# Interleaved weight tails, V returned from PSUM by ScalarE, and q spread one unit ahead

## The chip, the cores and the metric

The kernel runs on one core of one Trainium2 chip. The metric is device time in microseconds (us) of one launch. The engines named below are TensorE (PE, its weight loads PEld), VectorE (DVE), ScalarE (ACT), GpSimd (POOL) and SyncE (SP), which issues nearly all loads.

## The reference

One token for each of 8 sequences goes twice through an attention block with a cached K and V and a small MLP block. What matters, shortened:

```python
def _A_ref(x, k_cache, v_cache, wq, wo):        # x: 8 x 1 x 448, caches: 8 x 8 x 4096 x 256, bf16
    q = (x @ wq).reshape(B, 1, 16, 256)         # 2 query heads for each of 8 kv heads
    scores = einsum("bhqd,bhkd->bhqk", q, k) * 256 ** -0.5
    o = einsum("bhqk,bhkd->bhqd", softmax(scores), v)
    return o.reshape(B, 1, 4096) @ wo

def _B_ref(x, w1, w2, w3, w4):
    ...                                         # with one token the shifted part is zero: x1 = x
    return x1 + gelu(layernorm(x1) @ w3) @ w4

for _ in range(2):
    x = x + _A_ref(layernorm(x), k_cache, v_cache, wq, wo)
    x = x + _B_ref(layernorm(x), w1, w2, w3, w4)
```

Both passes use the same caches (268 MB in all) and the same weights. The second pass of a sequence needs its first one complete.

## The kernel before

**Units and chunks.** A unit is a pass (0 or 1), a sequence b (0 to 7) and a pair of kv heads gp (0 to 3). Its K and its V are four chunks each of 1 MB, 128 partitions of 8192 B. `places` holds 17 such chunks (`slots`, NC = 17). A K chunk is transposed in place by DVE in 32x32 blocks (`transpose_k`, L923, three instructions), multiplied with the spread q by PE into the PSUM tile `sc` (`scores`, L938), and goes through the exponential on ScalarE (`exps`, L947) into `p_n`. P is transposed by PE (L990), copied by ScalarE to `psv` (L997), and for each V chunk ScalarE copies the piece it needs to `ptw` (L1129). PE then multiplies it with V and adds up in `o` (`pv`, L1007). Two K chunks that lie in adjacent places are loaded with one 2 MB transfer (L860, rows of 16384 B) and scored by 32 matmuls 256 wide; otherwise there are two transfers of 1 MB (L891) and 64 matmuls 128 wide.

**What stays on the chip between the passes.** Of gp 2 and 3 of one sequence, 14 of 16 chunks stay in their places after pass 0 and are used again in pass 1. The other two are V chunks that go to PSUM: `inner` (unit gp 2, V chunk 1) to the banks `store0` to `store3`, and `part` (gp 3, V chunk 0), of which 6 of 16 rows go to `store4` and the second half of the bank of `sc`, while the rest sits in `rest`. DVE takes them there in pass 0 with block transposes (`away`, L958, and `part_away`, L979), and brings them back in pass 1 (`back`, L965, and `part_back`, L983) at the second K chunk of (1, b, 2). They go back into two K places that were kept free for this: that of K chunk 0 of (1, b, 2) and that of K chunk 2 of (1, b, 3).

**Order.** The list `items` has all chunk uses in order. It is worked through once, in Python, and each engine's instructions come in that order; `manual_schedule` means that nothing reorders them. A period belongs to one sequence b: its pass 1 on gp 3 and gp 2 from the kept chunks, then K and V of other units mixed (`block`), among them the pass 0 of b+1 on gp 2 and 3, and at the end only V chunks (`narrow`, loaded in two halves of 512 KB, L894), for which three places are left. Beside the narrow stretch runs the `chain`: the output projection of the sequence just finished, its MLP, its next q (`project_q`), in small steps given out by `step`. Each period is about 106 us long.

**Loads.** `emit_loads` is called after each item and issues loads on SP's queue in order while there are places. `place_for` looks for adjacent places for two K chunks and holds a load back for a place that is about to be freed (`held`). Eight DMA semaphores are used in turn, so at most eight loads are in flight.

**q.** For each unit pair (pass, b, half of gp), `give_q` calls `spread_q` at the first K chunk: four small matmuls (L370) into `misc`, then four DVE casts (L376) into one of four `qbds`.

**Weights with 448 rows.** 448 is three blocks of 128 rows and 64 more. `load_split` loads the three blocks (L193). The last 64 rows are cut in two halves by columns: the first goes to partitions 0 to 63, the second to 64 to 127, two loads (L913 for the blocks of wq that are loaded anew for `weights("q", rows)`, at three places in mid-run and one at the start; L1048 on SP's and L1049 on ScalarE's queue for the resident `wq_sb` and `w3_sb`). `wblk` and `q_of_block` choose x block 4 or 3, which have the last 64 values of x in the low or the high partitions and zeros in the others. `project_rows` (L350, L358) multiplies.

Of the kernel before, what the change touches and what calls it, by code (L numbers as in the profile page):

```python
# [17 lines left out]
def kernel(  # L18
# [80 lines left out]
    for u in range(2):  # L99
        nc.vector.tensor_reduce(  # L100
            usel[:, 2 * u : 2 * u + 2],
            ident.rearrange("p (k q h) -> p h k q", k=4, h=2)[:, :, :, 2 * u : 2 * u + 2],
            mybir.AxisListType.XY,
            ALU.add,
        )

    fold = consts.tile([128, 8], FP32, name="fold")
# [234 lines left out]

    def project_rows(w_of, half, r0, r1, ps):

        nb = r1 - r0
        for j in range(2):
            for h in range(HH):
                for fc in range(4):
                    w, xi = w_of(2 * h + j, fc)
                    nc.tensor.matmul(  # L350
                        ps[:, (j * HH + h) * nb : (j * HH + h + 1) * nb],
                        w,
                        xb[Bn][:, xi, r0:r1],
                        start=(fc == 0),
                        stop=(fc == 3),
                    )
        for j in range(2):
            nc.vector.tensor_copy(  # L358
                OT2[:, j, HH * half : HH * half + HH, r0:r1],
                ps[:, j * HH * nb : (j + 1) * HH * nb].rearrange("p (h b) -> p h b", b=nb),  # L360
            )

    def spread_q(b, half, qbd):
# [284 lines left out]
    AFTER = 10  # L648

    def block(k, v=None, slow=False):  # L650

        fresh = [(number[v], 1, c) for c in range(4)] if v else []
# [117 lines left out]
    def late(it):  # L770

        n, kv, c = it
        return kv == 0 and paired(n, c) and not (tasks[n][0] == 1 and stays(it))

    used_at = {it: k for k, it in enumerate(items)}
    for it in items:
# [5 lines left out]
    for b in range(Bn):  # L782
        again[(b, keep[0]), 0, 0] = again[(b, inner[0]), *inner[1:]]
        again[(b, keep[1]), 0, 2] = again[(b, part[0]), *part[1:]]
    free_at = [-1] * NC
# [59 lines left out]
    def emit_loads(most=None):  # L845
        n = 0
        while loads and places and n != most:
# [44 lines left out]
            else:  # L892
                for y in range(2):
                    nc.sync.dma_start(  # L894
                        dst[:, 8 * Dh * y : 8 * Dh * (y + 1)], src[:, 8 * Dh * y : 8 * Dh * (y + 1)]
                    )

    def load_weights(dst, kind, c):

        if kind == "o":  # L900
            nc.sync.dma_start(
                dst[:, 0 : WI * D].rearrange("p (h x) -> p h x", x=2 * D),
                A_wo[0 : WI * 128].rearrange("(h p j) d -> p h (j d)", p=128, j=2),
            )
        elif c == 0:
            nc.sync.dma_start(
                dst.rearrange("p (f c) -> p f c", f=2),
                A_wq[0:256, 0:HF].rearrange("(f p) c -> p f c", f=2),
            )
        else:  # L910
            nc.sync.dma_start(dst[:, 0:HF], A_wq[256:384, 0:HF])
            for k in range(2):
                nc.sync.dma_start(  # L913
                    dst[64 * k : 64 * k + 64, HF : HF + HF // 2],
                    A_wq[384:448, HF // 2 * k : HF // 2 * (k + 1)],
                )

# [36 lines left out]

    def away(slot):

        for n in range(4):
            nc.vector.transpose(  # L958
                store[n][:].bitcast(U32), slot[:].bitcast(U32)[:, 512 * n : 512 * n + 512]
            )  # L960

    def back(slot):

        for n in range(4):
            nc.vector.transpose(  # L965
                slot[:].bitcast(U32)[:, 512 * n : 512 * n + 512], store[n][:].bitcast(U32)
            )

    def part_words(slot):

        w = slot[:].bitcast(U32)
        return [
            (sc[:, 256 : 256 + 128 * (PR - 4)], w[:, 512 : 128 * PR]),
            (store[4][:], w[:, 0:512]),
        ]

    def part_away(slot):
        for kept_words, words in part_words(slot):
            nc.vector.transpose(kept_words.bitcast(U32), words)  # L979

    def part_back(slot):
        for kept_words, words in part_words(slot):
            nc.vector.transpose(words, kept_words.bitcast(U32))  # L983

# [56 lines left out]
    x_row = spare[1][:Bn, 256 : 256 + D]  # L1041
    nc.sync.dma_start(x_row, A_x.rearrange("b s d -> (b s) d"))
    emit_loads(2)
    ps0 = rows_to_cols(x_row, Bn)
    nc.vector.tensor_copy(xT[:], ps0)
    emit_loads(5)
    for t, src, cols in ((wq_sb, A_wq[:, HF:], HF), (w3_sb, B_w3, F)):
        nc.sync.dma_start(t[0:64, 3 * cols :], src[384:448, 0 : cols // 2])  # L1048
        nc.scalar.dma_start(t[64:128, 3 * cols :], src[384:448, cols // 2 : cols])  # L1049
    load_split(wq_sb, A_wq[:, HF:], HF)  # L1050
# [40 lines left out]

    def give_q(who):

# [16 lines left out]
        q_of[k] = who  # L1110
        run(spread_q(who[1], who[2], qbds[k]))

# [3 lines left out]
    v_items = [it for it in items if it[1] == 1]  # L1116
    v_next = dict(zip(v_items, v_items[1:]))
    plain = {it for it in v_items if (tasks[it[0]][:2] == (1, Bn - 1)) and tasks[it[0]][2] in free}

# [14 lines left out]
    for idx, it in enumerate(items):  # L1134
# [22 lines left out]
        if kv == 2:  # L1157
# [8 lines left out]
            elif c == 1:  # L1166
# [3 lines left out]
                def q_of_block(c, fc):  # L1170
                    if fc < 3:
                        t, at = (qw[0], fc * HF) if fc < 2 else (qw[1], 0)
                        return t[:, at + 128 * c : at + 128 * c + 128], fc
                    lo = 128 * c < HF // 2
                    at = HF + 128 * c - (0 if lo else HF // 2)
                    return qw[1][:, at : at + 128], 4 if lo else 3

# [4 lines left out]
                )  # L1182
                project_rows(q_of_block, 0, *rows, ps_q)
        elif kv == 0:
# [46 lines left out]
        else:  # L1231
            st = state[ps, b]
            if it in narrow and it[2] == 0 and not alone and any(e["kind"] == "chain" for e in gens):
                alone.append(n)
# [28 lines left out]
            else:  # L1263
                g8 = gp // 2
                if c == 0 and ("o", g8) not in st:
# [4 lines left out]
                if c == 0:  # L1270
                    o_of[n] = st["o", g8]
                o_now = o_of[n]
                if c == 0 and (alone_now or pairs_done.get((ps, b), 0) % 2 == 1):
                    done = pairs_done.get((ps, b), 0) + 1
# [24 lines left out]
                if ps == 0 and inside(it):  # L1299
                    away(slot)  # L1300
                if ps == 0 and halfway(it):
                    part_away(slot)
            if c == 3:
                pairs_done[ps, b] = pairs_done.get((ps, b), 0) + 1
# [15 lines left out]
        emit_loads()  # L1320
        step(idx, it in narrow)
    while gens:
# [159 lines left out]
```

## Time and profile before

| | us |
|---|---|
| median of three runs (lowest, highest) | 1060.6 (1059.31, 1061.72) |
| time of the profiled execution | 1061.44 |
| span of the profiled execution, first to last instruction | 1059.3 |
| PE busy (matmuls) / PEld | 632.2 / 401.6 |
| DVE busy | 617.0 |
| of it K transposes, L923 | 454.2 |
| of it V from PSUM, L965 and L983 | 28.7 |
| of it V to PSUM, L958 and L979 | 28.9 |
| ACT busy | 161.3 |

The span is what the profile covers; the execution's time has 2.1 us around it. Busy shares are means over stretches with different limits: none of the computing engines is above 60%, and the HBM traffic is 422.39 MB in the span. So the page's totals don't tell what sets the time; the slices and single stretches have to be read.

### The profile page before, as it was taken

Reading aid. Unit: us, or ns where it says so; the run is one execution under the profiler, and the core shown is the slowest. Engines: PE = TensorE matmul, PEld = TensorE weight load, DVE = VectorE, ACT = ScalarE, POOL = GpSimd, SP = SyncE. Lnnn points to the kernel's source line nnn. Section 1 sums busy time; section 2 is a strip of 40 time slices with the busy share of each in tenths; the row PEclk is TensorE's granted clock in tenths of the full one; section 3 lists DMA queues with packets and bytes.
Section 4 is the critical chain, followed back from the end, with each engine's and each line's share of the span. In section 5 each row is a group of like instructions: output and inputs, shape, how many; then the busy total and the mean of one; then the engine's idle time right before and its main releaser. Section 6 shows DMA issues by size and latency. Waiting matters only on the chain.

```text
span 1059.3 us, 29997 instructions
## 1 busy us (share of the span) xinstructions
PE 632.2 (60%) x13328; PEld 401.6 (38%) x13328; DVE 617.0 (58%) x1334; ACT 161.3 (15%) x615; POOL 16.3 (2%) x27
## 2 busy tenths in 40 slices
PE   3154454766476657754766576547664865576765
PEld 2032232543244424532434254324332543244544
DVE  5155567259725972597258825872588259724672
ACT  1011011121112121212111112111111121102110
POOL 0000000000000000000000000000000000000000
PEclk9999755775666555665665566757665665576665
DMA  9999999999999999999999999999999999999994
GB/s 303 389 420 424 422 420 420 394 416 423 418 388 416 420 415 332 409 423 419 395 394 420 421 377 410 423 421 404 377 424 422 392 417 422 419 398 392 418 418 187
DMA packets 72768, 424.32 MB, mean 401 GB/s; under 512 B 7608, under 2 KB 13632, under 8 KB 43456
## 3 DMA queue, kind: packets, MB, share of 16 engines
q1 hardware_dynamic: 72448, 422.17, 98.7%
q8 instruction: 104, 1.70, 0.6%
q10 hardware_dynamic: 192, 0.25, 0.1%
q14 instruction: 24, 0.20, 0.0%
HBM read 422.39 MB, written 0.01 MB: 399 GB/s over the span
## 4 chain that ended last, share of the span: by engine, by line
DMA 46%; DVE 26%; PE 21%; ACT 3%; issue 2%; SPq 1%; POOL 1%; DVEq 0%; ACTq 0%
DMA places<-in_A_v_cache_dram 30%; DVE places L923 20%; DMA places<-in_A_k_cache_dram 13%; PE sc L938 7%; PE o L1007 6%; PE misc L174 3%; ACT p_n L947 2%; DMA places<-in_A_wq_dram 2%; DVE store L958 2%; PE misc L529 1%; DVE qbd L376 1%; DMA places<-in_A_wo_dram 1%; DVE places L965 1%; SPq L193 1%; PE misc L350 0%
## 5 line engine op out<-in xcount | busy, mean ns | idle before, releaser
L923 DVE STREAM_TRANSPOSE places<-places 128x512 uint32<-128x512 uint32 (+1 forms) x576 | 454.2, 853 | 75.8 <-DMA places<-in_A_k_cache_dram 74.4
L938 PE MATMUL sc<-places,qbd 128*8 128x256 bf16 (+1 forms) x5344 | 248.4, 333 | 236.3 <-DVE places L923 227.8
L1007 PE MATMUL o<-places,ptw 128*8 128x256 bf16 x3808 | 233.2, 370 | 92.7 <-DMA places<-in_A_v_cache_dram 61.6
L938 PEld LDWEIGHTS <-qbd 128*8 128x8 bf16 x5344 | 134.8, 103 | 319.0 <-DVE places L923 140.8
L1007 PEld LDWEIGHTS <-ptw 128*8 128x8 bf16 x3968 | 103.1, 102 | 162.5 <-issue 83.0
L947 ACT ACTIVATE p_n<-sc 128x256 bf16<-128x256 f32 x128 | 95.2, 744 | 403.8 <-PE sc L938 403.8
L1129 ACT COPY ptw<-psv 128x32 bf16<-128x32 bf16 x248 | 51.9, 226 | 184.9 <-PE o L1007 180.5
L493 DVE RECIPROCAL rz<-misc 128x8 f32<-128x8 f32 (+1 forms) x37 | 6.8, 183 | 89.0 <-PE misc L490 89.0
L529 PE MATMUL misc<-R_t,o_sb 128*128 128x8 f32 (+1 forms) x140 | 29.8, 322 | 40.7 <-DVE R_t L515 35.4
L997 ACT CAST psv<-misc 128x128 bf16<-128x128 f32 x64 | 17.0, 265 | 236.3 <-PE misc L990 236.3
L529 PEld LDWEIGHTS misc<-R_t,o_sb 128*128 128x128 f32 x140 | 26.9, 268 | 51.0 <-issue 40.4
L376 DVE CAST qbd<-misc 32x32 bf16<-32x32 f32 x128 | 23.3, 182 | 37.1 <-PE misc L370 35.6
L947 ACT ACTIVATION_READ_ACCUMULATOR p_n<-sc 128x1 f32 x128 | 33.9, 265 | 0.0
L174 PEld LDWEIGHTS <-w_sb 128*128 128x128 bf16 x896 | 27.1, 100 | 16.5 <-issue 15.8
L525 DVE MEMSET o<- 128x256 f32 x35 | 9.5, 272 | 33.4 <-PE o L1007 30.9
L275 POOL TENSOR_TENSOR t<-t,nhalf 128x2 f32<-128x2 f32 (+2 forms) x18 | 12.0, 669 | 977.9 <-DVE t L296 977.9
L990 PE MATMUL misc<-identb,p_n 128*128 128x32 bf16 x256 | 18.0, 190 | 8.9 <-ACT p_n L947 6.8
L174 PEld LDWEIGHTS <-wo_sb 128*128 128x128 bf16 x704 | 20.9, 100 | 6.4 <-issue 6.4
L990 PEld LDWEIGHTS <-p_n 128*128 128x128 bf16 x256 | 11.8, 104 | 30.2 <-issue 18.7
L958 DVE STREAM_TRANSPOSE store<-places 128x512 uint32<-128x512 uint32 x32 | 19.7, 685 | 0.0
L965 DVE STREAM_TRANSPOSE places<-store 128x512 uint32<-128x512 uint32 x32 | 19.7, 674 | 0.0
L174 PE MATMUL misc<-xb,w_sb 128*128 128x32 bf16 x448 | 16.1, 187 | 4.9 <-DVE xb L304 4.8
(150 smaller groups left out, 348.8 us busy)
## 6 DMA issues: line engine op xcount, KB each, us to landing
places<-in_A_k_cache_dram SPq DMA_DIRECT2D x51, 2048.0 KB, 17.7
places<-in_A_v_cache_dram SPq DMA_DIRECT2D x194, 512.0 KB, 7.2
places<-in_A_k_cache_dram SPq DMA_DIRECT2D x90, 1024.0 KB, 13.4
places<-in_A_v_cache_dram SPq DMA_DIRECT2D x87, 1024.0 KB, 19.9
rest<-in_A_v_cache_dram SPq DMA_DIRECT2D x8, 640.0 KB, 18.4
places<-in_A_wo_dram SPq DMA_DIRECT2D x5, 896.0 KB, 19.7
places<-in_A_wq_dram SPq DMA_DIRECT2D x4, 1024.0 KB, 12.7
places<-in_A_v_cache_dram SPq DMA_DIRECT2D x8, 384.0 KB, 17.5
```

The costliest lines, as they stand in the source:

```text
L174: nc.tensor.matmul(bass.AP(out.tensor, out.offset, [out.ap[0], (1, WIDE)]), w, x.to_broadcast([128, WIDE]), start=start, stop=stop, skip_g ...
L376: nc.vector.tensor_copy(qbd[32 * a : 32 * a + 32, :, :, a, :], qs.rearrange("p e (f g u h) -> p (e f) u g h", f=2, u=2, h=2)[:, :, u],)
L529: nc.tensor.matmul(ot_ps[:, j], o_sb[:].rearrange("p (i j) -> p j i", j=2)[:, j], R, start=True, stop=True)
L923: nc.vector.transpose(w, w)
L938: nc.tensor.matmul(sc[32 * k : 32 * k + 8, 128 * (x % 2) : 128 * (x % 2 + nx)], qbd[:, ep, gp % 2].rearrange("p a h -> p (a h)"), v, start ...
L947: nc.scalar.activation(p_sb[:, :, :, 2 * u : 2 * u + 2].rearrange("p t i x -> p x t i"), sc[:, 0:256].rearrange("p (x t i) -> p x t i", x= ...
L958: nc.vector.transpose(store[n][:].bitcast(U32), slot[:].bitcast(U32)[:, 512 * n : 512 * n + 512])
L965: nc.vector.transpose(slot[:].bitcast(U32)[:, 512 * n : 512 * n + 512], store[n][:].bitcast(U32))
L990: nc.tensor.matmul(pt_ps[:, t], p_sb[:, t].rearrange("p i x -> p (i x)"), cols, start=True, stop=True,)
L997: nc.scalar.copy(p_to, pt_ps.rearrange("p t k (a h) -> p a (t k) h", a=4))
L1007: nc.tensor.matmul(o_ps[32 * q : 32 * q + 8, :], ptz[:, at : at + 8], v[:, y * Dh : (y + 1) * Dh] if v2 is None or y < PR else v2[:, (y - ...
L1129: nc.scalar.copy(ptw[:, ring_of[it], :, 6:8], psv[slot_of[it[0]]][:, it[2]])
```

## The change

Three parts, and what they need.

1. The last 64 rows of a weight are loaded in one transfer to 128 partitions: row r, halved by columns, goes to partitions 2r and 2r+1 (`load_tail`). For wq blocks loaded anew, the 64 values of x are doubled to match: `tail_cols` multiplies with a selector that DVE writes, and DVE masks the two halves by `parity` into `xq`. For the resident `wq_sb` and `w3_sb` the tails are loaded into place 13, and at item 12 PE sorts them into the layout of before, through PSUM, with ScalarE's copies (`sort_tail`). Place 13 joins the others then. x is loaded on ScalarE's queue.
2. `part` and `inner` are kept in PSUM as plain copies (`away`, a DVE bitwise OR with 0 on 32-bit words) and come back by ScalarE copies (`back`), of which one is issued after each item (`move`). They are used as the last V chunk of their units (`v_order`), and return to the places of the first two V chunks of (1, b, 3), no longer to two K places.
3. At the third K chunk of a unit, `q_ahead` issues the matmuls of the next q to be spread, and the casts follow at the fourth.

```diff
+    def tail_cols(r0, r1, ps):
+        nb = r1 - r0
+        two_t = chn.tile([128, Dh], FP32, tag="o_sb")
+        two = two_t[:, 0:64].bitcast(BF16)
+        nc.vector.tensor_copy(
+            two.rearrange("p (r k) -> p r k", k=2),
+            identb[:, 64:128].unsqueeze(2).to_broadcast([128, 64, 2]),
+        )
+        nc.tensor.matmul(ps, two, xb[Bn][:, 3, r0:r1], start=True, stop=True)
+        nc.vector.tensor_tensor(
+            xq[:, :, 0:nb],
+            ps.unsqueeze(1).to_broadcast([128, 2, nb]),
+            parity[:].unsqueeze(2).to_broadcast([128, 2, nb]),
+            ALU.mult,
+        )
+        return lambda xi: xb[Bn][:, xi, r0:r1] if xi < 3 else xq[:, xi - 3, 0:nb]
...
+    def v_order(v):
+        for chunk in (inner, part):
+            if v[0] == 1 and v[2] == chunk[0]:
+                return [c for c in range(4) if c != chunk[2]] + [chunk[2]]
+        return range(4)
...
-        again[(b, keep[0]), 0, 0] = again[(b, inner[0]), *inner[1:]]
-        again[(b, keep[1]), 0, 2] = again[(b, part[0]), *part[1:]]
+        again[(b, keep[1]), 1, homes[0]] = again[(b, part[0]), *part[1:]]
+        again[(b, keep[1]), 1, homes[1]] = again[(b, inner[0]), *inner[1:]]
...
+    def load_tail(dst, src):
+        nc.sync.dma_start(dst, src[D - 64 : D].rearrange("r (k c) -> r k c", k=2))
...
             nc.sync.dma_start(dst[:, 0:HF], A_wq[256:384, 0:HF])
-            for k in range(2):
-                nc.sync.dma_start(
-                    dst[64 * k : 64 * k + 64, HF : HF + HF // 2],
-                    A_wq[384:448, HF // 2 * k : HF // 2 * (k + 1)],
-                )
+            load_tail(dst[:, HF : HF + HF // 2], A_wq[:, 0:HF])
...
-            nc.vector.transpose(
-                store[n][:].bitcast(U32), slot[:].bitcast(U32)[:, 512 * n : 512 * n + 512]
-            )
...
-            nc.vector.transpose(
-                slot[:].bitcast(U32)[:, 512 * n : 512 * n + 512], store[n][:].bitcast(U32)
-            )
...
+    def inner_words(slot):
+        return [(store[n][:], slot[:, 1024 * n : 1024 * n + 1024]) for n in range(4)]
     def part_words(slot):
...
+            (store[4][:], slot[:, 0:1024]),
+            (sc[:, 256 : 256 + 128 * (PR - 4)], slot[:, 1024 : PR * Dh]),
...
+    def away(pieces):
+        for kept_words, words in pieces:
+            nc.vector.tensor_single_scalar(
+                kept_words.bitcast(U32), words.bitcast(U32), 0, op=ALU.bitwise_or
+            )
+    def back(kept_words, words):
+        nc.scalar.copy(words, kept_words.bitcast(BF16))
+    def move(all_of=False):
+        while moves:
+            back(*moves.pop(0))
+            if not all_of:
+                break
...
-    nc.sync.dma_start(x_row, A_x.rearrange("b s d -> (b s) d"))
+    nc.scalar.dma_start(x_row, A_x.rearrange("b s d -> (b s) d"))
+    tails = NC - 4
+    places.remove(tails)
...
-    for t, src, cols in ((wq_sb, A_wq[:, HF:], HF), (w3_sb, B_w3, F)):
-        nc.sync.dma_start(t[0:64, 3 * cols :], src[384:448, 0 : cols // 2])
-        nc.scalar.dma_start(t[64:128, 3 * cols :], src[384:448, cols // 2 : cols])
+    load_tail(slots[tails][:, 0 : HF // 2], A_wq[:, HF:])
+    load_tail(slots[tails][:, HF // 2 : HF // 2 + F // 2], B_w3)
+    def sort_tail(t, at, cols, banks):
+        n = cols // 4
+        for u in range(2):
+            for k in range(2):
+                nc.tensor.matmul(
+                    store[banks[u]][64 * k : 64 * k + 64, 0:n],
+                    identb[:, k:128:2],
+                    slots[tails][:, at + n * u : at + n * u + n],
...
+            nc.scalar.copy(
+                t[:, 3 * cols + n * u : 3 * cols + n * u + n], store[banks[u]][:, 0:n]
+            )
...
+    def q_ahead(idx):
+        seen = []
+        for m, kv, c in items[idx + 1 :]:
+            ps, b, gp = tasks[m]
+            if kv or m in seen or m == items[idx][0]:
+                continue
+            seen.append(m)
+            who = (ps, b, gp // 2)
+            if who in q_of:
+                if len(seen) == 2:
+                    return
+                continue
+            if ps == 1 and (gp in keep or b not in q_rows_done):
+                return
+            q_begun.append(give_q(who, True))
+            return
...
         if it == kept_q:
+            sort_tail(wq_sb, 0, HF, (1, 2))
+            sort_tail(w3_sb, HF // 2, F, (3, 4))
+            places.append(tails)
...
+            if c == 3 and q_begun:
+                run(q_begun.pop())
...
+            if c == 2:
+                q_ahead(idx)
...
-            if (ps, gp, c) == (1, keep[0], 1):
-                where[(b, part[0]), part[1:]] = part_place
-                part_back(slots[part_place])
-                where[(b, inner[0]), inner[1:]] = kept_place
-                back(slots[kept_place])
...
-            if (ps, gp, kv, c) == (1, keep[0], 0, 0):
-                kept_place = p
-            elif (ps, gp, kv, c) == (1, keep[1], 0, 2):
-                part_place = p
+            if (ps, gp, kv, c) == (1, keep[1], 1, homes[0]):
+                where[(b, part[0]), part[1:]] = p
+                moves.extend(part_words(slot))
+            elif (ps, gp, kv, c) == (1, keep[1], 1, homes[1]):
+                where[(b, inner[0]), inner[1:]] = p
+                moves.extend(inner_words(slot))
...
         emit_loads()
+        move()
```

More of the change, by code (lines that the diff above doesn't have):

```diff
@@ L105 @@
         )
+    parity = consts.tile([128, 2], FP32, name="parity")
+    nc.vector.tensor_reduce(
+        parity[:], ident.rearrange("p (m k) -> p k m", k=2), mybir.AxisListType.X, ALU.add
+    )
+    xq = consts.tile([128, 2, Bn], BF16, name="xq")
     fold = consts.tile([128, 8], FP32, name="fold")
@@ L341, in project_q, with project_rows @@
         yield
-    def project_rows(w_of, half, r0, r1, ps):
+    def project_rows(w_of, half, r0, r1, ps, cols=None):
         nb = r1 - r0
+        cols = xb[Bn][:, :, r0:r1] if cols is None else cols
         for j in range(2):
@@ L352, in project_rows @@
                         w,
-                        xb[Bn][:, xi, r0:r1],
+                        cols(xi) if callable(cols) else cols[:, xi, :],
                         start=(fc == 0),
@@ L648 @@
     AFTER = 10
+    def v_order(v):
[3 more added lines that the diff above has]
+        return range(4)
     def block(k, v=None, slow=False):
-        fresh = [(number[v], 1, c) for c in range(4)] if v else []
+        fresh = [(number[v], 1, c) for c in v_order(v)] if v else []
         if k is None:
@@ L773, in late @@
         return kv == 0 and paired(n, c) and not (tasks[n][0] == 1 and stays(it))
+    homes = v_order((1, 0, keep[1]))[:2]
+    assert part[0] == keep[1] and inner[0] == keep[0]
     used_at = {it: k for k, it in enumerate(items)}
@@ L953, in exps, with part_words @@
         )
-    def away(slot):
-        for n in range(4):
-            nc.vector.transpose(
-                store[n][:].bitcast(U32), slot[:].bitcast(U32)[:, 512 * n : 512 * n + 512]
-            )
-    def back(slot):
-        for n in range(4):
-            nc.vector.transpose(
-                slot[:].bitcast(U32)[:, 512 * n : 512 * n + 512], store[n][:].bitcast(U32)
-            )
[L969 to L983, printed above, removed]
+    def inner_words(slot):
+        return [(store[n][:], slot[:, 1024 * n : 1024 * n + 1024]) for n in range(4)]
+    def part_words(slot):
+        return [
+            (store[4][:], slot[:, 0:1024]),
+            (sc[:, 256 : 256 + 128 * (PR - 4)], slot[:, 1024 : PR * Dh]),
+        ]
+    def away(pieces):
+        for kept_words, words in pieces:
+            nc.vector.tensor_single_scalar(
+                kept_words.bitcast(U32), words.bitcast(U32), 0, op=ALU.bitwise_or
+            )
+    def back(kept_words, words):
+        nc.scalar.copy(words, kept_words.bitcast(BF16))
+    moves = []
+    def move(all_of=False):
[3 more added lines that the diff above has]
+                break
     def transpose_p(p_sb, p_to):
@@ L1046 @@
     emit_loads(5)
-    for t, src, cols in ((wq_sb, A_wq[:, HF:], HF), (w3_sb, B_w3, F)):
-        nc.sync.dma_start(t[0:64, 3 * cols :], src[384:448, 0 : cols // 2])
-        nc.scalar.dma_start(t[64:128, 3 * cols :], src[384:448, cols // 2 : cols])
+    load_tail(slots[tails][:, 0 : HF // 2], A_wq[:, HF:])
[8 more added lines that the diff above has]
+                    slots[tails][:, at + n * u : at + n * u + n],
+                    start=True,
+                    stop=True,
+                )
+            nc.scalar.copy(
+                t[:, 3 * cols + n * u : 3 * cols + n * u + n], store[banks[u]][:, 0:n]
+            )
     load_split(wq_sb, A_wq[:, HF:], HF)
@@ L1090, in step, with give_q @@
                     gens.remove(e)
-    def give_q(who):
+    q_rows_done = set()
+    q_begun = []
+    def q_ahead(idx):
[14 more added lines that the diff above has]
+            return
+    def give_q(who, begin=False):
         first = next((i[0] for i in items[now[0] :] if i[1] == 0), 0)
@@ L1110, in give_q @@
         q_of[k] = who
-        run(spread_q(who[1], who[2], qbds[k]))
+        g = spread_q(who[1], who[2], qbds[k])
+        if begin:
+            next(g)
+            return g
+        run(g)
     o_of = {}
@@ L1117 @@
     v_next = dict(zip(v_items, v_items[1:]))
+    v_last = {it[0]: it for it in v_items}
+    v_first = {it[0]: it for it in v_items[::-1]}
     plain = {it for it in v_items if (tasks[it[0]][:2] == (1, Bn - 1)) and tasks[it[0]][2] in free}
@@ L1173, in q_of_block @@
                         return t[:, at + 128 * c : at + 128 * c + 128], fc
-                    lo = 128 * c < HF // 2
-                    at = HF + 128 * c - (0 if lo else HF // 2)
-                    return qw[1][:, at : at + 128], 4 if lo else 3
+                    k = 2 * 128 * c // HF
+                    at = HF + 128 * c - k * HF // 2
+                    return qw[1][:, at : at + 128], 3 + k
                 ps_q = (
@@ L1182 @@
                 )
-                project_rows(q_of_block, 0, *rows, ps_q)
+                cols = tail_cols(*rows, misc[:, 320 : 320 + nb])
+                project_rows(q_of_block, 0, *rows, ps_q, cols)
+                if idx > 1:
+                    q_rows_done.update(range(*rows))
         elif kv == 0:
@@ L1225 @@
                     alone.clear()
-            if (ps, gp, c) == (1, keep[0], 1):
-                where[(b, part[0]), part[1:]] = part_place
-                part_back(slots[part_place])
-                where[(b, inner[0]), inner[1:]] = kept_place
-                back(slots[kept_place])
         else:
             st = state[ps, b]
+            if ps == 1 and (halfway(it) or inside(it)):
+                while moves and any(w.offset == v.offset for _, w in moves for _, v in (part_words if halfway(it) else inner_words)(slot)):
+                    move()
             if it in narrow and it[2] == 0 and not alone and any(e["kind"] == "chain" for e in gens):
@@ L1264 @@
                 g8 = gp // 2
-                if c == 0 and ("o", g8) not in st:
+                if it == v_first[n] and ("o", g8) not in st:
                     while not free_o:
@@ L1269 @@
                 alone_now = (ps, b) in split and gp in free
-                if c == 0:
+                if it == v_first[n]:
                     o_of[n] = st["o", g8]
                 o_now = o_of[n]
-                if c == 0 and (alone_now or pairs_done.get((ps, b), 0) % 2 == 1):
+                if it == v_first[n] and (alone_now or pairs_done.get((ps, b), 0) % 2 == 1):
                     done = pairs_done.get((ps, b), 0) + 1
@@ L1299 @@
                 if ps == 0 and inside(it):
-                    away(slot)
+                    away(inner_words(slot))
                 if ps == 0 and halfway(it):
-                    part_away(slot)
-            if c == 3:
+                    away(part_words(slot))
+            if it == v_last[n]:
                 pairs_done[ps, b] = pairs_done.get((ps, b), 0) + 1
@@ L1320 @@
         emit_loads()
+        move()
         step(idx, it in narrow)
```

## The prediction

> **What bounds the kernel now.** I read the page's slices first, then its DMA queues, stretches of the span by engine, the chain of waits around one restart, and the waits in total.
>
> ```profile
> DMA  9999999999999999999999999999999999999994
> GB/s 303 389 420 424 422 420 420 394 416 423 418 388 416 420 415 332 409 423 419 395 394 420 421 377 410 423 421 404 377 424 422 392 417 422 419 398 392 418 418 187
> q1 hardware_dynamic: 72448, 422.17, 98.7%
> ```
>
> The DMA engines are busy from end to end, and a full slice moves 418 to 424 GB/s. 424.32 MB at 422 GB/s would be 1005.5 us; the span is 1059.3. The packet records of the trace give a stricter floor. The median packet of 8192 B takes 312 ns, of 16384 B (two adjacent chunks in one row) 613 ns, of 4096 B 159 ns. All packets at their medians, over 16 engines, are 1021.6 us. Of the 37.7 us above that, some 5.4 lie in the first 12 us and 15.1 after 1038 us, where the last load lands and the closing products run. Some 17 us are lost in the middle, in dips; these are what a change can win.
>
> ```profile
> 22.00:28.00 6.00, 2.31 (x60) 1.15 (x48) 3.94 (x6) 0.74 (x2) 0.00 (x0) 1.00 1.03 268
> 345.00:395.00 50.00, 28.50 (x587) 17.25 (x578) 43.92 (x72) 9.23 (x33) 0.00 (x0) 0.57 1.01 419
> 395.00:410.00 15.00, 13.36 (x252) 8.62 (x248) 3.27 (x18) 1.98 (x10) 0.70 (x1) 0.50 0.86 285
> 545.00:550.00 5.00, 1.99 (x36) 1.29 (x37) 3.30 (x8) 0.71 (x5) 0.00 (x0) 0.50 1.06 311
> ```
>
> The columns are the stretch, its length, then busy time of PE, PEld, DVE, ACT and POOL, the granted clock, DMA share and GB/s. There are two kinds of dip. At 22 and 545 us the DMA share is full and the rate is low: packets are slow. At 395 us the share is 0.86: the engines have nothing to do, right after 50 us in which DVE was busy 43.9.
>
> ```profile
> 326.68 1.05 DVE places L983 x2
> 327.73 2.39 DVE places L965 x4
> ...
> 331.55 1.84 PE sc L938 x32
> ...
> 334.24 1.03 PE o L1007 x12
> 335.26 0.04 PE misc L370 x2
> ...
> 335.41 0.07 DVE qbd L376
> ...
> 336.21 9.37 DVE places L923 x12
> ```
>
> This is the chain of waits 60 us ahead of that second dip: start, length, what. K of the next units lands from 326 us on, but DVE first copies V back from PSUM (3.4 us). Then it waits until PE has scored and multiplied V and only then issued the four small products of L370, and it transposes the first K chunk at 336.2. A chunk takes DVE 2.4 us and the DMA engines 2.5, so these 9.5 us are hardly made good: from 385 to 394.8 us the loads wait for V places that late scores hold.
>
> ```profile
> L923 DVE STREAM_TRANSPOSE places<-places 128x512 uint32<-128x512 uint32 (+1 forms) x576 | 454.2, 853 | 75.8 <-DMA places<-in_A_k_cache_dram 74.4
> L965 DVE STREAM_TRANSPOSE places<-store 128x512 uint32<-128x512 uint32 x32 | 19.7, 674 | 0.0
> DVE qbd L376 <- PE misc L370: 35.6, 32, 4.0
> ```
>
> The last line is a wait: who for whom, us in total, times, longest. Of its 35.6 us, the gaps at 335, 547 and 759 us are 3.59 each.
>
> **The change, part by part.**
>
> *Interleaved tails.* The last 64 rows of a weight were two loads into 64 partitions each. Around them, at 8, 22, 545, 758 and 957 us, 2048 B packets take 123 to 138 ns on average against 84 for the quickest common ones, and the 8192 B packets beside them 370 to 450 instead of 312. Lost time from the rates: 4 us at 295 GB/s, 6 at 268, 5 at 311, 6 at 330, 6 at 315, against about 410 (386 at 22 us, where the neighbours are short): 1.1 + 1.8 + 1.2 + 1.2 + 1.4 = 6.7 us. Short packets alone don't do it: 1792 B packets that fill 128 partitions run at 79 ns between 28 and 40 us. The new load fills 128 partitions in one issue, so I take -6; bounds 0 (it wasn't the partitions) and -6.7.
>
> [...]
>
> *V back by ScalarE.* Away: of each unit pair, 6 DVE transposes become 6 bitwise copies, 48 in all. No row shows that operation. Nearest: the transpose into PSUM, 685 ns for 512 words; a DVE memset of 512, 485; TENSOR_SCALAR grows by 44 ns from 14 to 56 elements, so about 695. Bounds +0.5 to -9.6 us of DVE over the run; I take 0, by the row of its size. Back: 48 DVE transposes go (19.7 + 5.4 + 3.6 = 28.7 us of DVE), and ScalarE does 48 copies. Its copies take 226 ns for 32 elements, 265 for 128 and 395 for 256, so 0.75 to 1.0 ns per element: 0.97 to 1.24 us for 1024, 0.59 to 0.72 for 512. That is 5.5 to 6.9 us in each of 8 periods, 44 to 55 in all. ScalarE is busy 161 us of 1059, and each period's copies fall where 8 to 14 loads are out or landed ahead of use, over 20 us of cover at 2.5 us a load. I take 0; uncovered it is the slow rival.
>
> *Order of V.* The chunks held in PSUM are used last of their units, and their homes are the V places freed first, no longer two K places. The place plan, read off both kernels' code, emits 97 loads at an earlier item (mostly 2 to 5 items, right after the narrow stretch) and 37 later (by up to 4). It helps the restart; priced below. The plan also finds fewer adjacent places: 39 loads of 2 MB instead of 51. Each broken pair costs 128 packets x (2x312-613 = 11 ns)/16 = 0.09 us, so +1.1 us. PE gets 608 more weight loads and matmuls, 19 score pairs of 64 instructions instead of 32: about 0.7 us each at the half clock (24 take 0.98 us and 32 wide ones 1.90), 13 us in all. PE is 60% busy and waits 228 us for L923 at this line, so 0 on the path; bounds 0 and +13.
>
> *q spread ahead.* Its four products and four casts (182 ns) are issued during the third and fourth K chunk of the unit in front. At the restart DVE then no longer stands behind PE's V product: from the chain, the 3.4 us of the back and some 1.8 (exponential 0.74, V product 1.03) go, 5.2 of the 9.5; later gaps such as 1.81 at 372 us go too.
>
> What 5 to 7 us of lead per period are worth is bounded by what the DMA engines lose when DVE is late, since a lead beyond that only waits for loads. By rates against 400 GB/s: 395 to 410 at 285, 4.3 us; 190 to 200 at 367, 505 to 515 at 369 and 612 to 622 at 365, 0.8 to 0.9 each; 764 to 769 at 347, 0.7. Sum 7.5. The loads there are of 4096 B and three deep, a part that stays; I take -6, bounds 0 and -7.5. If DVE gave back nothing, the lateness would stay and this is 0.
>
> *Small additions.* Three times in mid-run, ahead of a q projection, DVE copies a 128x128 selector (227 ns as a cast at the start), PE multiplies, DVE masks (170 ns), and PE's projection stands behind it: about 0.4 us of DVE and a round trip each, with all DVE transposes queued behind the mask. +0.5, bounds 0 and +3 (the 3.6 us gap is the longest such round trip, and the L358 wait there is 5.3 at most already). The sorting of the tails at 62 us, 8 matmuls and 4 ScalarE copies of about 0.6 us, lies where PE is idle half of the time and SP waits for earlier loads; 0, and 5 if it weren't covered. x goes by ScalarE's queue, so SP's first weight load moves up 0.45 us; the 240 KB which that queue carried in the first 8 us now stand in SP's, 0.57 us at 420 GB/s. One place fewer until item 12 delays loads by one item while eight are in flight. Together 0.
>
> Sum: -6 + 1.1 - 6 + 0.5 = -10.4 us on the profiled span of 1059.3, that is 1048.9. The profiled execution took 1061.4, the runs' median is 1060.6, 1.3 above the span: **1050.2, said as 1050**.
>
> **Rivals.**
>
> *ScalarE becomes the wait (slower).* Six copies stand in one queue with the P copies (L1129) and exponentials (L947) that PE waits for, right at the restart, and PE then frees places late. Against: the loads ahead, and 403.8 us that the exponentials wait for PE. It decides once the delay per period passes DVE's lead. If half of 5.5 us comes through at each restart and PE's lag costs the lead as well, 8 x 2.75 = 22, no gain from DVE: 1060.6 + 22 - 6 + 1.6 = 1078; at a quarter 1067.
>
> *DVE's lead is hidden.* The dips belong to the narrow stretch itself (three places, 7.2 us to land). Then -6 + 1.6: 1056. For it: 410 to 425 us still runs at 386 GB/s with DVE idle. Against: the 0.86 share.
>
> *The tails stay slow.* The packets may be slow for the weights' rows in memory, and the load then only looks different: -6 + 1.6, 1056 as well. Against: slow neighbours of another tensor.
>
> *All dips close.* 1021.6 + 1.1, the start 4.4, the end 15.1: span 1042.2, 1043.5. For it: the loads emitted earlier. Against: the three-place stretch is untouched.
>
> **Chances.** Forecast (1046 to 1054) 0.47; all dips close 0.11; lead hidden 0.13; tails slow 0.07; ScalarE the wait 0.15; no change 0.07, gains and added waits cancelling. 0.2% is 2.1 us, about what this kernel's measurement can tell from none. Faster 0.78, same 0.07, slower 0.15. Range 1043 to 1061: the floor below, and above it the smaller gains, the added costs at their upper ends and no change.
>
> **What would show it.** Rates near 400 at the five tails, with 2048 B packets near 84 ns. No DVE row from PSUM to places; L376's successor waiting well below 35.6 us; first transposes of the restart about 5 us sooner; share above 0.95 in what is now 395 to 410 us. DVE near 590 us busy, ACT 205 to 216. Wrong: ACT waits of V products of several us per period, or P copies late by 1 us at each; a span of full packets that is still 1055.

## The result, and the profile after

The changed kernel takes 1048.82 us (median; 1048.5 to 1049.37), beside 1060.69 for the kernel before on the same chip. The ratio is 0.9885, 95% interval 0.9865 to 0.9906: 12.2 us faster by the ratio, 11.9 by the medians. The span of the profiled execution fell from 1059.3 to 1047.3 us.

The slices and the main queue on the page of the changed kernel:

```profile
DMA  9999999999999999999999999999999999999994
GB/s 356 395 421 421 422 422 420 387 420 418 419 398 419 421 417 396 416 423 416 386 418 425 418 395 416 420 417 383 416 422 418 404 414 422 417 378 404 418 419 193
q1 hardware_dynamic: 74224, 422.41, 99.0%
```

The first slice rose from 303 to 356 GB/s, and the slice that was the deepest dip in mid-run from 332 to 396; the lowest slice in mid-run is now 378. One dip in each period stays: the narrow stretch with three places.

The same stages by stretch (stretch, length, busy PE, PEld, DVE, ACT, POOL, granted clock, DMA share, GB/s), changed kernel; times here are up to 12 us earlier than before:

```profile
20.00:24.00 4.00, 1.59 (x44) 0.89 (x35) 3.79 (x8) 0.74 (x2) 0.00 (x0) 1.00 1.01 393
340.00:390.00 50.00, 26.15 (x511) 14.77 (x515) 42.16 (x66) 8.82 (x31) 0.00 (x0) 0.60 1.01 419
390.00:405.00 15.00, 12.46 (x294) 8.02 (x286) 3.56 (x20) 1.92 (x9) 0.70 (x1) 0.73 1.03 398
537.00:542.00 5.00, 3.52 (x156) 2.77 (x155) 5.00 (x7) 4.37 (x10) 0.00 (x0) 0.87 1.03 416
```

The first and the last line are the stretches in which the tails' packets move (20.2 to 22.7 us and 537.1 to 540.0 us). Both kinds of dip are gone: 268 became 393 GB/s at the resident tails, 311 became 416 at the first reload of wq. The entry into the narrow stretch, 0.86 share at 285 GB/s, now has a full share at 398.

The restart, in the chain of waits of the changed kernel (start, length, what):

```profile
322.41 0.74 ACT p_n L981 x2
...
324.43 1.81 PE sc L972 x31
326.24 0.12 PE misc L395 x4
...
326.48 0.17 DVE qbd L401
...
327.27 2.08 DVE places L957 x3
```

From the end of the first exponential here to the first transpose it is 4.1 us (327.27 - 323.15). In the kernel before that exponential ended at 326.66 and the transpose began at 336.21, 9.55 us later. The gain is 5.4 us, beside the 5.2 that the prediction worked out.

The loads of the narrow stretch feel it. Before it starts, they wait until DVE has copied `part` away to PSUM, which stands behind DVE's transposes and the scores. This wait of SP's queue, before and after (who for whom, us in total, times, longest):

```profile
SPq L894 <- DVE store L979: 52.8, 8, 9.0
```

```profile
SPq L928 <- DVE sc L1003: 44.1, 8, 5.6
```

Groups of the changed kernel (busy us, mean ns | idle before), then a wait (total, times, longest):

```profile
L1008 ACT COPY places<-store 128x1024 bf16<-128x1024 bf16 x40 | 40.2, 1027 | 5.0 <-PE o L1040 4.6
L1003 DVE TENSOR_SCALAR store<-places 128x512 uint32<-128x512 uint32 x40 | 25.0, 679 | 0.2
DVE qbd L401 <- PE misc L395: 32.4, 14, 9.9
```

With 4.7 us for the half pieces, the copies back take ScalarE 44.9 us. The bitwise copy takes 679 ns where the transpose took 685. The last line did not fall as I said it would.

Where the time went can be added up from the packet records: in each microsecond, the packets moved, at the median duration of their size, over 16 engines; what is missing to a full microsecond is lost. In us, for the profiled executions:

```
                 packets   lost at    lost at    lost in    lost in     span
                           0 to 12    12 to 40   between    last 22
before            1021.6     5.4        1.8       16.2       14.4      1059.3
changed           1023.0     3.7       -0.7        7.4       13.9      1047.3
tails alone       1022.0     3.7       -0.7       16.0       13.3      1054.3
V alone           1022.9     5.0        1.7       11.3       14.3      1055.2
q ahead alone     1021.6     5.4        1.6       12.3       14.2      1055.0
without tails     1022.9     5.1        1.8       11.3       14.3      1055.3
1 MB loads        1026.8     3.6       -0.7        8.6       12.9      1051.2
```

(A negative loss means packets a little quicker than the median.) Of the 12.0 us, 4.2 come from the first 40 us, 8.8 from the middle and 0.5 from the end; 1.4 are given back by smaller packets. The profiled executions of the tails alone (1056.46 us, median 1058.8) and of the copies back on VectorE (1050.71, median 1053.19) were the quickest of their kernels, so their traces show less than the medians.

Two more sums from the same records tell the kinds of loss apart. While the tails' packets are under way, the packets take 8.1 us more than at their medians in the kernel before (2.0 for the tails' own packets, 6.0 for the 4096 and 8192 B packets beside them) and 0.2 us in the changed kernel. And the microseconds of the middle in which the DMA share is below 0.9 lose about 4.4 us before, 8.4 with the tails alone, 1.0 with V alone, 2.0 with q ahead alone, 1.6 without tails and 0.5 in the changed kernel.

### The profile page after: what moved, and what is told of

Same layout as the page of the kernel before. It is cut to its first block, busy times and chain, and to the rows that moved or that the text cites. A ratio compares the mean times of both kernels' runs of the same rounds, so it can differ in the third digit from the quotient of the medians.

```text
span 1047.3 us, 31277 instructions
## 1 busy us (share of the span) xinstructions
PE 643.9 (61%) x13948; PEld 415.8 (40%) x13948; DVE 592.5 (57%) x1295; ACT 203.8 (19%) x667; POOL 16.3 (2%) x27
## 4 chain that ended last, share of the span: by engine, by line
DMA 55%; PE 21%; DVE 16%; ACT 3%; issue 3%; SPq 1%; POOL 1%; DVEq 0%; ACTq 0%; POOLq 0%
DMA places<-in_A_v_cache_dram 31%; DMA places<-in_A_k_cache_dram 24%; DVE places L957 11%; PE sc L972 7%; PE o L1040 6%; PE misc L180 4%; DVE store L1003 2%; ACT p_n L981 2%; PE misc L554 2%; DVE qbd L401 1%; SPq L199 1%; POOL t L281 1%; PE misc L357 1%; ACT o_sb L548 1%; PE misc L515 0%
## 5 line engine op out<-in xcount | busy, mean ns | idle before, releaser
L972 PE MATMUL sc<-places,qbd 128*8 128x128 bf16 (+1 forms) x5952 | 256.1, 321 | 219.7 <-DVE places L957 205.5
L972 PEld LDWEIGHTS <-qbd 128*8 128x8 bf16 x5952 | 147.2, 103 | 301.7 <-DVE places L957 123.8
L401 DVE CAST qbd<-misc 32x32 bf16<-32x32 f32 x128 | 22.7, 178 | 33.7 <-PE misc L395 32.4
L1008 ACT COPY places<-store 128x1024 bf16<-128x1024 bf16 x40 | 40.2, 1027 | 5.0 <-PE o L1040 4.6
L180 PEld LDWEIGHTS <-w_sb 128*128 128x128 bf16 x896 | 27.3, 101 | 17.4 <-issue 16.2
L1003 DVE TENSOR_SCALAR store<-places 128x512 uint32<-128x512 uint32 x40 | 25.0, 679 | 0.2
L1023 PEld LDWEIGHTS <-p_n 128*128 128x128 bf16 x256 | 11.8, 105 | 28.0 <-issue 16.5
L515 PE MATMUL misc<-zm,one 128*128 128x8 f32 (+1 forms) x74 | 18.3, 319 | 4.4 <-DVE zm L507 3.0
```

What stands on the lines that cost most here:

```text
L180: nc.tensor.matmul(bass.AP(out.tensor, out.offset, [out.ap[0], (1, WIDE)]), w, x.to_broadcast([128, WIDE]), start=start, stop=stop, skip_g ...
L401: nc.vector.tensor_copy(qbd[32 * a : 32 * a + 32, :, :, a, :], qs.rearrange("p e (f g u h) -> p (e f) u g h", f=2, u=2, h=2)[:, :, u],)
L972: nc.tensor.matmul(sc[32 * k : 32 * k + 8, 128 * (x % 2) : 128 * (x % 2 + nx)], qbd[:, ep, gp % 2].rearrange("p a h -> p (a h)"), v, start ...
L1003: nc.vector.tensor_single_scalar(kept_words.bitcast(U32), words.bitcast(U32), 0, op=ALU.bitwise_or)
L1008: nc.scalar.copy(words, kept_words.bitcast(BF16))
L1023: nc.tensor.matmul(pt_ps[:, t], p_sb[:, t].rearrange("p i x -> p (i x)"), cols, start=True, stop=True,)
```

## The experiments

All ratios are to the kernel before on the same chip. The three parts, each alone and each left out:

| parts in the kernel | ratio | 95% interval | us of 1060.6 |
|---|---|---|---|
| tails | 0.9981 | 0.9966 to 0.9995 | -2.0 |
| V by ScalarE, order, homes | 0.9978 | 0.9961 to 0.9995 | -2.3 |
| q ahead | 0.9966 | 0.9949 to 0.9983 | -3.6 |
| tails and V | 0.9889 | 0.9873 to 0.9906 | -11.8 |
| tails and q ahead | 0.9936 | 0.9918 to 0.9954 | -6.8 |
| V and q ahead | 0.9976 | 0.9959 to 0.9993 | -2.5 |
| all three | 0.9885 | 0.9865 to 0.9906 | -12.2 |

**Tails alone.** The kernel before with `tail_cols`, `load_tail` and `sort_tail`, and with what belongs to them (x on ScalarE's queue, place 13 held back at the start):

```diff
-            for k in range(2):
-                nc.sync.dma_start(
-                    dst[64 * k : 64 * k + 64, HF : HF + HF // 2],
-                    A_wq[384:448, HF // 2 * k : HF // 2 * (k + 1)],
-                )
+            load_tail(dst[:, HF : HF + HF // 2], A_wq[:, 0:HF])
```

> The kernel before with the interleaved tails alone. My theory (64-partition loads slow all packets beside them): 6 us faster than before, about 1054.5; the 2048 B packets average below 95 ns instead of 131, and the rates at the five tails are near 400 GB/s. Rival (the packets are slow for the rows in memory, not for the partitions): packets stay at 125 to 140 ns and the time within 1.5 us of before. Second rival (DMA time won there is lost again at the next DVE-late entry into the narrow stretch): packets at 84 ns, but under 3 us faster.

Measured: 1058.8 us; 2048 B packets fell from 129 to 86 ns on average. The same rows of the same tensors now come at 86 ns a packet, so the rows in memory were not the cause; what differs is that one load fills 128 partitions where two filled 64 each. But the time is the second rival's. Two entries into the narrow stretch, by stretch:

```profile
390.00:405.00 15.00, 11.52 (x224) 7.60 (x224) 4.03 (x19) 2.94 (x13) 0.70 (x1) 0.61 0.81 265
760.00:770.00 10.00, 8.30 (x215) 5.96 (x204) 6.05 (x14) 2.14 (x9) 0.00 (x0) 0.67 0.76 302
```

The DMA engines run dry more than before (0.81 for 0.86). Loads that arrive sooner wait for the same late DVE. The table of losses says it in one row: the start keeps its 4.2 us, and the middle stays at 16.0, though the slow packets in it are gone. What they gave back turns into idle time: the loss at a share below 0.9 rises from 4.4 to 8.4 us.

**V alone.** The kernel before with `v_order`, the new homes, bitwise `away`, and:

```diff
-    nc.vector.transpose(words, kept_words.bitcast(U32))
+    nc.scalar.copy(words, kept_words.bitcast(BF16))
```

> The kernel before with V returned by ScalarE, the new order of V and the new homes, no other part. My theory: DVE loses the 28.7 us of the back and starts the first transposes of a restart 3.4 us sooner; with the broken pairs (+1.1 us) 3 us faster than before, about 1057.5. Rival (ScalarE becomes the wait): slower than before by 3 us or more, with P copies late. Rival (DVE's lead is hidden): 1 us slower, from the broken pairs.

Measured: 1057.77 us. The gain is 2.3 us by the ratio with the broken pairs in it; ScalarE does not become the wait.

**q ahead alone.** The kernel before with `q_ahead`:

```diff
+            if c == 3 and q_begun:
+                run(q_begun.pop())
...
+            if c == 2:
+                q_ahead(idx)
```

> The kernel before with q spread ahead alone. My theory: the 3.6 us waits at three restarts and the later 1.8 us ones go, the V copies of DVE stay; 2 us faster than before, about 1058.5. Rival (lead hidden): no change within 1 us.

Measured: 1056.57 us, 3.6 faster by the ratio, more than expected.

**Tails left out.** The changed kernel with the loads into 64 partitions, without `tail_cols` and `sort_tail`:

```diff
-            load_tail(dst[:, HF : HF + HF // 2], A_wq[:, 0:HF])
+            for k in range(2):
+                nc.sync.dma_start(
+                    dst[64 * k : 64 * k + 64, HF : HF + HF // 2],
...
-    load_tail(slots[tails][:, 0 : HF // 2], A_wq[:, HF:])
-    load_tail(slots[tails][:, HF // 2 : HF // 2 + F // 2], B_w3)
+    for t, src, cols in ((wq_sb, A_wq[:, HF:], HF), (w3_sb, B_w3, F)):
+        nc.sync.dma_start(t[0:64, 3 * cols :], src[384:448, 0 : cols // 2])
+        nc.scalar.dma_start(t[64:128, 3 * cols :], src[384:448, cols // 2 : cols])
```

> The changed kernel with the tails loaded into 64 partitions as before. In the kernel before the interleaved tails alone gave 1.6 us, though 2048 B packets fell from 129 to 86 ns. My theory (late DVE took the rest back, and in the changed kernel DVE is in time, so that DMA time won is kept): 6 us slower than the changed kernel's 1048.8, about 1055; 2048 B packets at 129 ns again. Rival (tails are worth the 1.6 us in any company): 1050.5.

Measured: 1057.65 us, slower than the changed kernel by 8.8 us by the medians and 9.7 by the ratios; 2048 B packets at 124 ns. Two of its reloads of wq, by stretch:

```profile
540.00:546.00 6.00, 3.03 (x117) 2.41 (x110) 4.24 (x8) 3.94 (x9) 0.00 (x0) 0.89 1.04 326
952.00:958.00 6.00, 4.70 (x102) 3.38 (x92) 1.90 (x10) 2.17 (x7) 0.00 (x0) 1.00 1.00 282
```

Full share, low rate, as before. So the same edit is worth 2 us where DVE is late and 9 to 10 where it is not (5.0 and 8.0 by the spans of the profiled executions).

**V left out.** The changed kernel with DVE's transposes back into K places, the old order of V and the old homes:

```diff
+            if (ps, gp, c) == (1, keep[0], 1):
+                where[(b, part[0]), part[1:]] = part_place
+                part_back(slots[part_place])
+                where[(b, inner[0]), inner[1:]] = kept_place
+                back(slots[kept_place])
...
-        move()
```

> The changed kernel with V returned by DVE into the two K places as before. My theory (lead of DVE, less the broken pairs): 2.5 to 4 us slower than 1048.8, about 1052; DMA share below 1 again at some entries of the narrow stretch. Rival (once q is ahead, DVE has lead enough): within 1 us or faster by the 1.1 us of the broken pairs.

Measured: 1053.13 us, slower by 4.3 us by the medians and 5.4 by the ratios. The rival falls: q ahead alone does not give lead enough. One entry ran dry again:

```profile
750.00:760.00 10.00, 7.87 (x181) 4.83 (x173) 9.58 (x15) 1.84 (x7) 0.00 (x0) 0.53 0.82 314
```

DVE is busy 9.58 of 10 us there, and the share is 0.82.

**q ahead left out.** The changed kernel with `q_ahead` and its calls removed:

```diff
-            if c == 3 and q_begun:
-                run(q_begun.pop())
...
-            if c == 2:
-                q_ahead(idx)
```

> The changed kernel without q spread ahead: casts and their wait stand at the first K chunk of a unit. My theory: 3 to 4.5 us slower than 1048.8, about 1052.5, with the waits of DVE on the spreading products back at restarts. Rival (once V comes back by ScalarE, DVE has lead enough): within 1 us.

Measured: 1049.09 us, 0.3 slower and inside the interval. Here the rival holds and my theory falls. Its wait on the products, and its restart in the chain of waits:

```profile
DVE qbd L401 <- PE misc L395: 35.1, 31, 4.0
```

```profile
317.59 9.80 DMA places<-in_A_k_cache_dram
...
327.43 0.18 DVE qbd L401
...
328.04 2.97 DVE places L957 x4
```

The waits are nearly all back, yet the first transpose starts at 328.04, against 327.27 with q ahead. The chain names the landing of K at 327.39, a load issued at 317.6. The wait on the products had ended just before (the first cast starts at 327.24), so by the chain casts ahead of time could have gained some 0.65 us here. This one restart doesn't settle the cause, since TensorE was granted 1.00 of its clock from 324 to 328 us and 0.50 in the changed kernel, where the 32 score matmuls took 1.88 us instead of 1.05. But over all eight restarts the first transpose comes 0.4 us later in the mean, at one of them 2.9 us later (535.68 for 532.74), and the DMA engines don't run dry: a share below 0.9 costs 0.5 us in both kernels. Once V comes back by ScalarE, DVE has lead enough.

**Copies back on VectorE.** The changed kernel, same order and homes:

```diff
-        nc.scalar.copy(words, kept_words.bitcast(BF16))
+        nc.vector.tensor_single_scalar(words.bitcast(U32), kept_words.bitcast(U32), 0, op=ALU.bitwise_or)
```

> The changed kernel with the 48 copies back issued on VectorE instead of ScalarE, in the same places of the order and to the same homes. My theory (DVE's time at the restart counts): DVE gains about 28 us of work and 1.5 to 3 us of the gain are lost, about 1051. Rival (order and homes did it, the engine doesn't matter): within 1 us of the changed kernel's 1048.8. Rival (ScalarE hurts): faster than 1048.

Measured: 1053.19 us (ratio 0.9932, 0.9906 to 0.9957), 5.0 slower by the ratio, more than expected (1.6 in the profiled executions). A group of it, and the entry into the narrow stretch:

```profile
L1008 DVE TENSOR_SCALAR places<-store 128x512 uint32<-128x512 uint32 x40 | 26.1, 668 | 5.5 <-PE o L1042 5.5
```

```profile
390.00:405.00 15.00, 12.53 (x296) 8.63 (x296) 3.44 (x19) 2.07 (x11) 0.70 (x1) 0.77 0.92 338
```

The engine matters: 26.1 us of DVE and 5.5 of its waiting, set between K transposes, bring back a share below 1. Leaving out part 2 as a whole costs 5.4 us by the ratios, so what the new order and the new homes give by themselves is not told apart from nothing.

**ScalarE's copies fourfold and twice.** In the changed kernel, `back` issues the same copy four times or, in a later run, twice:

```diff
         nc.scalar.copy(words, kept_words.bitcast(BF16))
+        nc.scalar.copy(words, kept_words.bitcast(BF16))
```

> The changed kernel with each of ScalarE's 48 copies from PSUM issued four times over (the same values), so 16.7 us more of ScalarE's queue in each period instead of 5.6 once. My theory (the copies are covered by loads ahead): once they are free; fourfold they exceed what lies between P copies and cost something, 2 to 8 us, about 1053. Rival (ScalarE's copies already cost part of their 45 us): 20 us or more slower, above 1069, as the cost would grow in proportion.

> The changed kernel with each of ScalarE's 48 copies issued twice. Fourfold cost 52 us for 135 us of added copies. My theory (a knee: what fits between P copies is free, so once is free): twice costs under 4 us, 1049 to 1053. Rival (cost in proportion from the first copy on, so that the changed kernel already pays): 17 us slower, about 1066.

Measured: 1101.36 us (1.0385, 1.0357 to 1.0413) for fourfold, 53 slower; 1049.86 (0.9896, 0.9875 to 0.9917) for twice, 1.2 slower by the ratio and within the intervals. One wait, of the changed kernel and of fourfold:

```profile
PE o L1040 <- ACT ptw L1207: 28.9, 35, 1.4
```

```profile
PE o L1043 <- ACT ptw L1210: 103.2, 41, 6.0
```

With the copies issued twice this wait is 50.2 us in total, and hardly any of it reaches the time. There is a knee, though fourfold went far beyond the 2 to 8 us that I expected. At 45 and 90 us of copies the cover holds; at 180 us, V products wait up to 6 us for P copies. The mechanism of the slow rival exists; the changed kernel is at least a factor of two away from it.

**Loads of 1 MB only.** The changed kernel with each 2 MB load as two:

```diff
-                nc.sync.dma_start(
-                    places_t[:, p * PB : (p + 2) * PB],
+                for q, i in ((p, it), (p + 1, mate)):
+                    nc.sync.dma_start(
+                        slots[q],
...
-                    .rearrange("(p u z) d -> u p (z d)", u=2, z=32)[it[2] // 2],
+                        .rearrange("(p x y) d -> x p (y d)", x=4, y=16)[i[2]],
```

> The changed kernel with its 39 loads of 2 MB (rows of 16384 B) cut into two of 1 MB (rows of 8192 B) to the same places; the scores are unchanged. By my price of a broken pair, 0.09 us: 39 x 0.09 = 3.5 us slower than 1048.8, about 1052. Rival (packet size costs nothing on the path): within 1 us.

Measured: 1052.95 us (0.9926, 0.9907 to 0.9945), 4.3 slower by the ratio, 0.11 us a pair. The K loads of the changed kernel and of this one (count, KB each, us to landing):

```profile
places<-in_A_k_cache_dram SPq DMA_DIRECT2D x114, 1024.0 KB, 19.7
...
places<-in_A_k_cache_dram SPq DMA_DIRECT2D x39, 2048.0 KB, 19.2
```

```profile
places<-in_A_k_cache_dram SPq DMA_DIRECT2D x192, 1024.0 KB, 18.4
```

The packets' floor rose by 3.8 us and the span by 3.9. With DVE in time, packet size is paid in full.

**More pairs.** If pairs pay, a planner that looks further for neighbours should win a little:

```diff
-    AHEAD = 4
-    QUEUED = 7
+    AHEAD = 6
+    QUEUED = 6
```

> The changed kernel with the planner's QUEUED at 5 instead of 7, which plans more adjacent places: 60 of 84 K pairs side by side instead of 51. My theory: 0.5 to 1 us faster than 1048.8, about 1048. Rival (loads are held back for the neighbour and that costs more): slower than 1050.

> The changed kernel with the planner's AHEAD at 6 instead of 4 and QUEUED at 6 instead of 7: 68 of 84 K pairs side by side, against 51 in the changed kernel and 60 in the run with QUEUED 5; loads are held back longer for a neighbour. My theory: the packets' floor falls by another 1 us, and the longer holds give about that back, 1047.5 to 1049. Rival (holds starve the queue): above 1050.

Measured: 1048.33 us (0.9876, 0.9856 to 0.9896) with QUEUED 5 alone, 54 loads of 2 MB; 1046.17 (0.9859, 0.9835 to 0.9883) with both, 55 such loads, 1.3 us below the range that I expected. Of the 60 and 68 pairs planned, 54 and 55 became loads of 2 MB, so the second floor fell by far less than the 1 us more that I expected: the floors are 1021.2 and 1021.0 us, 1.8 and 2.0 below the changed kernel's. The second is the quickest kernel of the study, faster than before beyond doubt. Against the changed kernel the intervals overlap, so that step isn't shown, only in line with the floor.

## Why the prediction was right, point by point

The forecast was 1050 us, the measurement 1048.8. The sum held, with errors that partly cancelled, and that it came so near is partly luck. It added two gains of 6 us as if each stood by itself; by that account the tails alone should have given 6 us and V with q ahead 5, and they gave 2.0 and 2.5. The bound of 17 us to win in the middle was in truth 18.0, because 0.7 us of the 15.1 put at the end lay behind the last instruction.

**Tails, taken at -6: 7.8 in the losses, 8.8 or 9.7 when left out.** The reading was right: same bytes, full rate, packets at 85 ns. The term was too small at the start: I took 2.9 us off the two dips there, and beside the kernel without tails the first 40 us gave 3.9 (in it the first weight load, issued at 0.74 instead of 1.19 us). The three reloads in mid-run were priced at 3.8. While their tails land, the changed kernel moves 416, 413 and 390 GB/s (537 to 542, 747 to 752 and 948 to 952 us), and the middle lost 7.4 us instead of 11.3 without tails, so that price can stand. What I missed is the condition. Alone the edit gives 2 us, because the time it frees is lost again wherever DVE is late. I had put the two gains side by side as if each stood by itself. Most of the loss was in neighbours that fill 128 partitions: of the 8.1 us of slow packets, 6.0 are theirs, and while the tail at 545 us was under way 8192 B packets took 440 ns on average instead of 312.

**Lead of DVE, taken at -6: 4.9 in the losses.** Between 40 us and the last 22, losses fell by 8.8; less 3.9 for the reloads, 4.9 are left, as much as V and q ahead give without the tails (16.2 to 11.3). The size was near; the division of the work was not. Of the 5.2 us at the restart I gave 3.4 to the copies and 1.8 to q. Beside the other two, q ahead is worth 0.3 us, within the interval, though alone it gives 3.6. It and the copies back are partly two ways to the same lead: the two together, without the tails, give 2.5 us, no more than either alone (their intervals overlap). Beside V by ScalarE there is nothing left for q ahead to win.

**Broken pairs, +1.1.** Confirmed: 0.09 us a pair was reckoned, 0.11 measured with 39 pairs, so 1.3 for the 12.

**ScalarE's copies, 0 on the path.** Confirmed, within 1.2 us, by the copies made twice. 44.9 us of work lies near the lower end of the predicted 44 to 55; from the 226 ns of a copy of 32 bf16 values to the 1027 of one of 1024 it is 0.81 ns for each further value.

**Away and PE's extra matmuls, 0.** The bitwise copy, 679 ns for 512 words, is as long as the transpose, 685. PE rose by 11.7 us busy (13 reckoned). DVE is busy 592.5 us (near 590 forecast), ACT 203.8 (205 to 216). Neither term was tried alone.

**Small additions, +0.5.** Not seen in the losses and not tried alone. They may be anything small, below zero too.

**The wait of L376, said to fall well below 35.6: wrong.** It is 32.4 us. It has 14 instances instead of 32, and three of 8.7 to 9.9 us at 318, 526 and 737. There DVE has nothing else to do in the narrow stretch (it is busy for less than 0.1 us of each) and comes early to its next instruction, and the DMA share stays at 0.99 to 1.04. These long waits were no cost, so a total over the run could not be the test; the start of the first transpose was.

**The rivals.** ScalarE as the wait needs more than twice the copies; four times are enough. "Lead hidden" and "tails slow" fall with the single parts left out. "All dips close" stays out of reach: 7.4 us are still lost in the middle. They lie in the narrow stretches, where most bytes come in 4096 B packets (99% from 390 to 405 us, at 398 GB/s), as 386 to 400 GB/s there suggested.

## What to carry to other kernels

When a transfer-bound kernel also has an engine that comes late, two small fixes can each look nearly worthless alone and be worth far more together (here 2.0 and 2.3 us alone, 11.8 together); leave each out of the full version before dropping it, and also to find the one that has become idle (here the q spread ahead). Read low transfer rates by their share: here full share with a low rate (1.03 at 268 GB/s) was slow packets, and a share below 1 (0.86 at 285 GB/s) a late consumer. Beside the loads that filled only half the partitions, 8192 B packets took 440 to 548 ns on average instead of 312.

## What the runs showed of the hardware

- While loads into 64 partitions are in flight, 2048 B packets take 124 to 129 ns on average over the run, and 85 when the load fills 128 partitions; 8192 B packets that fill 128 partitions slow down beside them (440 to 548 ns on average in the kernel before, between the first and the last packet of such a tail, instead of 312).
- Time of a packet grows a little slower than its size: 159 ns for 4096 B, 312 for 8192, 613 for 16384. 39 transfers of 2 MB cut in two cost 4.3 us in 1060.
- ScalarE copies 1024 bf16 values per partition from PSUM in 1027 ns and 512 in 592. VectorE needs 668 ns for 512 32-bit words from PSUM, which hold the same data as 1024 bf16 values, and 679 ns into it; so VectorE would be quicker for the piece, and the kernel is still 5.0 us slower with it there.
